# Local softmax's sums from a column of ones beside the values, one result tile of two banks, and GpSimd's value copies in eight pieces

## The chip, the cores and the metric

The kernel runs on one core of a Trainium2 chip. The metric is the time of one execution on the device, in microseconds (us). The engines are named as in the profile: PE is TensorE (PEld its weight loads), DVE is VectorE, ACT is ScalarE, POOL is GpSimd, SP is SyncE, which only issues DMAs here.

## The reference

Attention over 8 batches, 8 heads, 576 positions and 64 dimensions, in fp32; then a mixture of experts over the 4608 resulting rows of 512. Heads 0 to 3 are local (a row sees itself and the 31 positions before it), heads 4 to 7 are strided (a row sees earlier positions that are equal to it modulo 32).

```
scores = scale * np.matmul(q, k.transpose(0, 1, 3, 2))
mask_local = (rel >= 0) & (rel < stride)
mask_strided = (rel >= 0) & (pos[None, :] % stride == pos[:, None] % stride)
scores = np.where(masks[None, :, :, :], scores, -1000000000.0)
scores = scores - np.max(scores, axis=-1, keepdims=True)
attn = np.exp(scores)
attn = attn / (np.sum(attn, axis=-1, keepdims=True) + 1e-09)
out = np.matmul(attn, v)
...
logits = x @ w_gate
expert_idx = np.argmax(logits, axis=1)
...
    h = np.maximum(x_sorted[lo:hi] @ w1[e], 0.0)
    y_sorted[lo:hi] = h @ w2[e]
```

Each row of the expert stage is scaled by its gate's softmax weight and put back in its own place.

## The kernel before, in words

Attention takes roughly the first 235 us; the experts follow. Attention is a pipeline of 40 chunks, five in a batch, in the order strided, local, strided, local, local (list `ch`, line 650). A local chunk has 256 rows (the last of a batch 64) of the four local heads, in blocks of 32 rows that each see 64 keys: their own 32 and the 32 before. The loop of line 687 runs one step n for each chunk and interleaves the stages of neighbouring chunks; the order in which the code is written is the order on every engine, as nothing is reordered afterwards.

For a local chunk the stages are, with the step at which each stands relative to the chunk's own: scores (`qkl`, PE, one step ahead), row maxima and subtraction (`sml_a`, lines 306 and 307, DVE, one step ahead), the exponential (`sml_x`, line 312, ACT), the sums of the exponentials, 1e-9 and the reciprocals (`sml_b`, lines 317 to 319, DVE, at the end of the chunk's own step), transposes of the exponentials (`ptl`, line 326 on PE and 328 on ACT, one step later), the product with the values (`avl`, line 344 on PE, two steps later) and, on DVE, the result times the reciprocal into the row tile `xr` (line 349, one instruction for each parity of the heads). Three steps later `otl` transposes the rows for the gate (line 362 on PE, 364 on ACT) and `rows_out` adds the strided heads' columns (lines 377 and 378) and stores the rows. So line 349 is followed in the next step by line 362.

The strided chunks go through `sms_a` (lines 238, 239), `sms_x` (243), `sms_b` (248 to 253, which ends in DVE's transpose `pts`), `sms_c` (260 on DVE, 262 on ACT) and `avs` (273 on PE; 278 on DVE or 280 on ACT move its result).

The results of `avl` and `avs` both lie in PSUM tiles `o` of one bank each, two of them in turn. Transposes go through three PSUM tiles `t`, so a PE transpose can wait for whoever reads the tile used three allocations before.

The local values of a batch lie in `VL[b % 2]` (tile `vl` or `xg`): 18 blocks of 32 positions for each of two pairs of heads. A partition group holds the block's own keys (rows `own`) and the block before it (rows `prev`). `load_vl` brings the own rows by DMA, issued by SP; `load_prev` (line 120) lets POOL copy them, one block on, to the `prev` rows, with one copy of 2176 elements per parity, thus two a batch. In POOL's program these two copies stand after the ranking work of an earlier batch (lines 499 to 525) and before that of the next.

Once a batch, in the same step as `load_prev`, the ranking of an earlier batch begins: the gate's logits, transposed on PE (line 431), are summed on DVE (432, 440), DVE subtracts the maxima (442, tile `rw`), and ACT takes their exponential (444). On ACT this exponential stands ahead of line 328 of the running step. Later DVE steps of the ranking are 445 to 449 and 472 to 488; PE's part are lines 457 to 470 and 530. At the end of attention the last chunks are interleaved with the splits of the first expert's weights (573 on ACT, 574 on DVE), with padding counts (461 to 466), and with the first tiles of the experts, for which `hidden` also uses the PSUM tiles of attention.

Of the kernel before, what the change touches and what calls it, by code (L numbers as in the profile page):

```python
# [8 lines left out]
F32 = mybir.dt.float32  # L9
# [4 lines left out]
OP = mybir.AluOpType  # L14
# [9 lines left out]
DM = H * D  # L24
NTOK = B * S
# [15 lines left out]
def kernel(ctx, tc, q, k, v, w_gate, w1, w2, out):  # L41
# [7 lines left out]
    XA, XB = (keep.tile([128, n], F32, name=nm) for nm, n in (("x1", 4096), ("xg", 2 * NB * D)))  # L49
# [15 lines left out]
    VL = [p0.tile([128, 2, NB, D], F32, name="vl"),  # L65
# [41 lines left out]
    def load_vl(b):  # L107
        t = VL[b % 2]
        for par in range(2):

            own = slice(64 * par + 32, 64 * par + 64)
            for hp in range(2):
                nc.sync.dma_start(t[own, hp], bass.AP(tensor=v.tensor, offset=base(v, b, 2 * hp + par),
                                                      ap=[[D, 32], [32 * D, NB], [1, D]]))

    def load_prev(b):
        t = VL[b % 2]
        for par in range(2):
            own, prev = slice(64 * par + 32, 64 * par + 64), slice(64 * par, 64 * par + 32)
            G.tensor_copy(t[prev, :, 1:], t[own, :, :NB - 1])  # L120
# [50 lines left out]
    V.memset(VL[0][:, :, 0:1], 0.0)  # L171
# [10 lines left out]
    SC = psk.tile([128, 2, 2, 256], F32, name="sc")  # L182
    QTS, PS, PL, PT, OL, XS, XL, RL = ({} for _ in range(8))
# [80 lines left out]
    def avs(b, c):  # L264
# [3 lines left out]
        for hp in range(2):  # L268
            p = ps.tile([128, 4, 4, NB], F32, name="o", bufs=2)
# [30 lines left out]
    def sml_a(b, g):  # L300
        n = 8 if g < 2 else 4
        s = PL.pop((b, g)).rearrange("p a j h c -> p a (j h) c")
        mx = RL[b, g] = wk.tile([128, 8, 2], F32, name="mxl", bufs=4)
        p = PT[b, g] = wk.tile([128, 8, 64], F32, name="pl", bufs=3)
        two = lambda t: t[:, :n].rearrange("p (x a) c -> p a x c", a=2)
        V.tensor_reduce(two(mx)[:, :, :, 0], s, axis=AX.X, op=OP.max)
        V.tensor_tensor(two(p), s, two(mx)[:, :, :, 0:1].to_broadcast([128, 2, n // 2, 64]), op=OP.subtract)
# [5 lines left out]

    def sml_b(b, g):
        n = 8 if g < 2 else 4
        mx, p = RL[b, g], PT[b, g]
        V.tensor_reduce(mx[:, :n, 0], p[:, :n], axis=AX.X, op=OP.add)
        V.tensor_scalar(mx[:, :n, 0], mx[:, :n, 0], 1e-9, None, op0=OP.add)
        V.reciprocal(mx[:, :n, 1], mx[:, :n, 0])
# [11 lines left out]
    def avl(b, g):  # L331
# [3 lines left out]
        mx = RL.pop((b, g))  # L335
        o = OL[b, g] = wk.tile([128, 2, DM], F32, name="xr", bufs=3)
        ps2 = [ps.tile([128, 2, 2, D], F32, name="o", bufs=2) for par in range(2)]
        for jj in range(nj):
            for hp in range(2):
                for j in range(nq):  # L340
                    blk = 8 * g + 4 * jj + j
                    for par in range(2):
                        r = slice(64 * par, 64 * par + 64)
                        T.matmul(ps2[par][32 * j:32 * j + 32, jj, hp], pt[r, 2 * jj + hp, 32 * j:32 * j + 32],  # L344
                                 VL[b % 2][r, hp, blk], start=True, stop=True)
            if jj == 0: yield
        for par in range(2):
            rs = mx.rearrange("p (j a h) e -> p j a h e", a=2, h=2)[:rows, :nj, :, par, 1:2]
            V.tensor_tensor(o[:, :, :4 * D].rearrange("p j (a h d) -> p j a h d", a=2, h=2)[:rows, :nj, :, par], ps2[par][:rows, :nj],
                            rs.to_broadcast([rows, nj, 2, D]), op=OP.mult)  # L350
# [336 lines left out]
    for n in range(-1, N + 3):  # L687
# [26 lines left out]
        if n == 0:  # L714
            V.memset(VL[1][:, :, 0:1], 0.0)
# [42 lines left out]
        at(n, sms_b, sml_b)  # L758
# [25 lines left out]
    def hidden():  # L784

        for f in range(8):
            p = ps.tile([128, C0], F32, name="o", bufs=2) if f % 2 else SC[:, f // 2 % 2, 0]
# [71 lines left out]
    z = [ps.tile([TM, DM], F32, name="o", bufs=2) for t in range(N0)]  # L859
# [235 lines left out]
```

## Time and profile before

| | |
|---|---|
| median of 3 runs | 692.95 us |
| lowest, highest run | 689.67, 693.1 us |
| the profiled execution | 693.73 us, of which the span of its instructions is 691.9 us |
| mean granted TensorE clock | 0.971 |
| busy share PE, DVE, ACT, POOL over the span | 92%, 50%, 44%, 28% |
| a full batch of attention (113.6 to 137.7 us) | PE 21.82, DVE 21.32, ACT 16.32, POOL 10.81 of 24.10 us |

All lines of the trace are from the one profiled execution. A row of the timeline reads: start in us from the span's start, duration in us, engine, line, operation, output and inputs by the names of the tiles with shapes, how many instructions are merged into the row, and in square brackets how long the engine sat idle before it and for whom. "issue" there means that the profile shows nothing that was waited for. A row of groups reads: line, engine, operation, tiles, shapes, count | busy us in all, mean ns of one | idle time before them. A row of the windows gives the length of a stretch and the busy time of each engine in it, then the granted clock, the share of the DMA engines and GB/s.

### The profile page before, as it was taken

What the parts mean: (1) busy time and instruction counts of PE and PEld (TensorE: products, weight loads), DVE (VectorE), ACT (ScalarE), POOL (GpSimd) and SP (SyncE); (2) the same over time, 40 slices, a digit from 0 to 9 for tenths busy, and PEclk for the clock granted to TensorE, in tenths of its full rate; (3) what the DMA queues carried; (4) which work ended last, traced back from release to release, by engine and by line L of the source; (5) the groups of instructions that cost most, each with busy time, mean ns of one, the idle gap of its engine ahead of it and who ended that gap; (6) DMA issues with size and microseconds to landing.
All of it is one profiled execution on the core that took longest, in us unless ns stands there. A gap on an engine that the chain in (4) does not pass through costs nothing.

```text
span 691.9 us, 18307 instructions
## 1 busy us (share of the span) xinstructions
PE 637.9 (92%) x7558; PEld 552.7 (80%) x7558; DVE 345.3 (50%) x766; ACT 307.2 (44%) x596; POOL 196.6 (28%) x263
## 2 busy tenths in 40 slices
PE   6678989988977989999999999999998999999995
PEld 4556666766656869999899799889997998999994
DVE  5866889886898653343334243443331542414210
ACT  6547756764764342433433243432441542434211
POOL 0222245425435570060140060141043041103002
PEclk9899999999996999999999999999999999999998
DMA  8898677868655271380470470561435343231001
GB/s 189 182 212 206 173 204 184 216 183 187 145 182 164 71 267 42 93 282 22 162 224 1 140 247 29 164 206 31 139 97 185 99 144 122 66 108 68 17 17 56
DMA packets 91029, 95.59 MB, mean 138 GB/s; under 512 B 62158, under 2 KB 64206, under 8 KB 90833
## 3 DMA queue, kind: packets, MB, share of 16 engines
q1 hardware_dynamic: 83152, 71.34, 37.6%
q0 software_dynamic: 7680, 22.03, 9.1%
q8 instruction: 75, 1.23, 0.8%
q14 instruction: 122, 0.99, 0.5%
HBM read 74.47 MB, written 22.02 MB: 139 GB/s over the span
## 4 chain that ended last, share of the span: by engine, by line
PE 70%; issue 11%; DVE 7%; ACT 5%; DMA 3%; POOL 2%; SPq 2%; POOLq 0%; ACTq 0%; DVEq 0%
PE h L623 8%; PE h L625 8%; PE h L624 8%; PE y L641 5%; PE y L642 5%; PE y L643 5%; PE t L613 2%; PE y L897 2%; PE y L895 2%; PE y L896 2%; PE t L201 2%; PE o L273 2%; PE o L344 2%; PE z L641 2%; PE z L642 2%
## 5 line engine op out<-in xcount | busy, mean ns | idle before, releaser
L884 POOL DMA_INDIRECT out_dram<-yo,idx x48 | 54.8, 1142 | 293.8 <-ACT yo L647 176.7
L630 DVE SCALAR_TENSOR_TENSOR h1l<-h,h1h 128x256 fp32r<-128x256 f32 (+3 forms) x64 | 32.8, 512 | 122.7 <-ACT h1h L629 122.7
L623 PE MATMUL h<-x,w1h 128*128 128x256 f32 (+3 forms) x256 | 82.2, 321 | 0.8 <-ACT yo L647 0.8
L625 PE MATMUL h<-x,w1l 128*128 128x256 f32 (+3 forms) x256 | 80.9, 316 | 0.0
L624 PE MATMUL h<-x,w1h 128*128 128x256 f32 (+3 forms) x256 | 80.9, 316 | 0.0
L629 ACT ACTIVATE h1h<-h 128x256 fp32r<-128x256 f32 (+3 forms) x64 | 29.1, 454 | 104.7 <-PE h L625 88.0
L603 POOL DMA_INDIRECT xg<-xrows,src x48 | 53.7, 1118 | 49.7 <-PE h L623 29.7
L623 PE MATMUL h<-x0h,w1h 128*128 128x256 f32 x224 | 63.6, 284 | 0.3 <-ACT yo L647 0.3
L624 PE MATMUL h<-x0l,w1h 128*128 128x256 f32 x224 | 63.4, 283 | 0.0
L625 PE MATMUL h<-x0h,w1l 128*128 128x256 f32 x224 | 63.4, 283 | 0.0
L630 DVE SCALAR_TENSOR_TENSOR h0l<-h,h0h 128x256 fp32r<-128x256 f32 x56 | 23.3, 420 | 72.3 <-ACT h0h L629 72.3
L574 DVE TENSOR_TENSOR w1l<-stg,w1h 128x1024 fp32r<-128x1024 f32 x32 | 38.7, 1229 | 24.6 <-ACT w1h L573 24.6
L623 PEld LDWEIGHTS h<-x,w1h 128*128 128x128 f32 x256 | 48.1, 188 | 1.6 <-issue 1.2
L624 PEld LDWEIGHTS h<-x,w1h 128*128 128x128 f32 x256 | 48.1, 188 | 0.3
L625 PEld LDWEIGHTS h<-x,w1l 128*128 128x128 f32 x256 | 48.0, 188 | 0.0
L580 DVE TENSOR_TENSOR w<-stg,w 128x1024 fp32r<-128x1024 f32 x32 | 38.9, 1221 | 12.4 <-ACT w L579 12.4
L623 PEld LDWEIGHTS h<-x0h,w1h 128*128 128x128 f32 x224 | 42.9, 192 | 0.9 <-ACT yo L647 0.5
L624 PEld LDWEIGHTS h<-x0l,w1h 128*128 128x128 f32 x224 | 42.9, 192 | 0.3
L625 PEld LDWEIGHTS h<-x0h,w1l 128*128 128x128 f32 x224 | 43.0, 192 | 0.0
L647 ACT ACTIVATE yo<-y,gw 128x512 f32<-128x512 f32 (+2 forms) x26 | 17.8, 685 | 51.7 <-PE y L643 47.0
L641 PE MATMUL y<-w,h1h 128*128 128x512 f32 (+1 forms) x96 | 38.9, 406 | 0.0
L895 PE MATMUL y<-h1h,w 128*128 128x288 f32 (+1 forms) x128 | 38.6, 301 | 0.0
(243 smaller groups left out, 1592.5 us busy)
## 6 DMA issues: line engine op xcount, KB each, us to landing
stg<-in_moe_w_dram SPq DMA_DIRECT2D x64, 512.0 KB
xrows<-xr SPq DMA_DIRECT2D x16, 512.0 KB
qs<-in_q_dram SPq DMA_DIRECT2D x8, 512.0 KB
ks<-in_k_dram SPq DMA_DIRECT2D x8, 512.0 KB
ql<-in_q_dram SPq DMA_DIRECT2D x32, 128.0 KB
kl<-in_k_dram SPq DMA_DIRECT2D x32, 128.0 KB
vs<-in_v_dram SPq DMA_DIRECT2D x16, 144.0 KB
vl<-in_v_dram SPq DMA_DIRECT2D x16, 144.0 KB
```

The source lines that it names most:

```text
L574: V.tensor_tensor(l[:, i], t, h[:, i].bitcast(F32), op=OP.subtract)
L580: V.tensor_tensor(l, t, h.bitcast(F32), op=OP.subtract)
L603: G.indirect_dma_start(out=XG[t], out_offset=None, in_=x_out[:rows, :], in_offset=bass.IndirectOffsetOnAxis(ap=src[:, NT * e + t:NT * e + ...
L623: T.matmul(p, W1H[:, c, fs], x[0][:, c, :n], start=(c == 0), stop=False)
L624: T.matmul(p, W1H[:, c, fs], x[1][:, c, :n], start=False, stop=False)
L625: T.matmul(p, W1L[:, c, fs], x[0][:, c, :n], start=False, stop=(c == 3))
L630: V.scalar_tensor_tensor(h[1][:, f, :n], p, 0.0, h[0][:, f, :n].bitcast(F32), op0=OP.max, op1=OP.subtract)
L641: T.matmul(p, h[0][:, f, cs], W2H[:, f], start=(f == 0), stop=False)
L642: T.matmul(p, h[1][:, f, cs], W2H[:, f], start=False, stop=False)
L643: T.matmul(p, h[0][:, f, cs], W2L[:, f], start=False, stop=(f == 7))
L884: i = G.indirect_dma_start(out=out, out_offset=bass.IndirectOffsetOnAxis(ap=idx[:, c:c + 1], axis=0), in_=YO[t], in_offset=None, bounds_ch ...
L895: T.matmul(p, W2H[:, f, ds_], H1[0][:, f, cs], start=(f == 0), stop=False)
```

## The change

Three things are changed, all around the local heads' product with the values.

1. A value row gets a 65th element that is one (`DV = D + 1`). `VL` has rows of 65; the ones are written once by a memset for each of the two tiles, and the DMAs bring only the first 64. The product's moving operand has 65 columns, so its last column is the sum of the exponentials. `sml_b` is gone, with its three DVE instructions per local chunk. In `avl`, between the product and the two multiplications, DVE now adds 1e-9 to the sums in PSUM (one instruction for both parities) and takes the reciprocals.
2. The two PSUM tiles `o` become one tile `oo` of two banks that is held throughout; the strided product, `hidden` and the first expert's `z` take its halves in the same turn as before.
3. `load_prev` makes eight copies a batch, of nine or eight blocks (585 or 520 elements), in place of two of 2176.

```
+DV = D + 1
...
-    XA, XB = (keep.tile([128, n], F32, name=nm) for nm, n in (("x1", 4096), ("xg", 2 * NB * D)))
+    XA, XB = (keep.tile([128, n], F32, name=nm) for nm, n in (("x1", 4096), ("xg", 2 * NB * DV)))
...
-    VL = [p0.tile([128, 2, NB, D], F32, name="vl"),
+    VL = [p0.tile([128, 2, NB, DV], F32, name="vl"),
...
-                nc.sync.dma_start(t[own, hp], bass.AP(tensor=v.tensor, offset=base(v, b, 2 * hp + par),
+                nc.sync.dma_start(t[own, hp, :, :D], bass.AP(tensor=v.tensor, offset=base(v, b, 2 * hp + par),
...
-            G.tensor_copy(t[prev, :, 1:], t[own, :, :NB - 1])
+            for hp in range(2):
+                for j in (1, 10):
+                    n = min(9, NB - j)
+                    G.tensor_copy(t[prev, hp, j:j + n], t[own, hp, j - 1:j + n - 1])
...
-    V.memset(VL[0][:, :, 0:1], 0.0)
+    V.memset(VL[0][:, :, 0:1, :D], 0.0)
+    V.memset(VL[0][:, :, :, D:], 1.0)
...
+    OO = psk.tile([128, 2, 512], F32, name="oo")
...
-            p = ps.tile([128, 4, 4, NB], F32, name="o", bufs=2)
+            p = OO[:, hp, :16 * NB].rearrange("p (e x i) -> p e x i", e=4, x=4)
...
-    def sml_b(b, g):
-        n = 8 if g < 2 else 4
-        mx, p = RL[b, g], PT[b, g]
-        V.tensor_reduce(mx[:, :n, 0], p[:, :n], axis=AX.X, op=OP.add)
-        V.tensor_scalar(mx[:, :n, 0], mx[:, :n, 0], 1e-9, None, op0=OP.add)
-        V.reciprocal(mx[:, :n, 1], mx[:, :n, 0])
...
-        ps2 = [ps.tile([128, 2, 2, D], F32, name="o", bufs=2) for par in range(2)]
+        ps2 = OO[:, :, :4 * DV].rearrange("p a (j h d) -> p a j h d", j=2, h=2)
...
-                        T.matmul(ps2[par][32 * j:32 * j + 32, jj, hp], pt[r, 2 * jj + hp, 32 * j:32 * j + 32],
+                        T.matmul(ps2[32 * j:32 * j + 32, par, jj, hp], pt[r, 2 * jj + hp, 32 * j:32 * j + 32],
                                  VL[b % 2][r, hp, blk], start=True, stop=True)
...
+        rs = wk.tile([128, 2, 2, 2, 2], F32, name="rs")
+        sm, rc = rs[:rows, 0, :, :nj], rs[:rows, 1, :, :nj]
+        V.tensor_scalar(sm, ps2[:rows, :, :nj, :, D], 1e-9, None, op0=OP.add)
+        V.reciprocal(rc, sm)
         for par in range(2):
-            rs = mx.rearrange("p (j a h) e -> p j a h e", a=2, h=2)[:rows, :nj, :, par, 1:2]
-            V.tensor_tensor(o[:, :, :4 * D].rearrange("p j (a h d) -> p j a h d", a=2, h=2)[:rows, :nj, :, par], ps2[par][:rows, :nj],
-                            rs.to_broadcast([rows, nj, 2, D]), op=OP.mult)
+            V.tensor_tensor(o[:, :, :4 * D].rearrange("p j (a h d) -> p j a h d", a=2, h=2)[:rows, :nj, :, par],
+                            ps2[:rows, par, :nj, :, :D], rc[:, par, :, :, None].to_broadcast([rows, nj, 2, D]), op=OP.mult)
...
-        at(n, sms_b, sml_b)
+        at(n, sms_b, None)
...
-            p = ps.tile([128, C0], F32, name="o", bufs=2) if f % 2 else SC[:, f // 2 % 2, 0]
+            p = OO[:, f // 2 % 2, :C0] if f % 2 else SC[:, f // 2 % 2, 0]
...
-    z = [ps.tile([TM, DM], F32, name="o", bufs=2) for t in range(N0)]
+    z = [OO[:, t] for t in range(N0)]
```

The first place where the order moves is DVE, in the step whose local result is transposed on PE right after it; `xr` is that result's row tile, `mxl` and `rs` hold maxima, sums and reciprocals, and `sc` the next scores. Before:

```order
L306 TENSOR_REDUCE mxl<-sc 128x2x2
L307 TENSOR_TENSOR pl<-sc,mxl 128x2x2x64
L349 TENSOR_TENSOR xr<-o,mxl 128x2x2x64 x2
L317 TENSOR_REDUCE mxl<-pl 128x8
L318 TENSOR_SCALAR mxl<-mxl 128x8
L319 RECIPROCAL mxl<-mxl 128x8
L238 TENSOR_REDUCE mxs<-sc 128x16
```

And on DVE at the same place in the changed kernel, whose lines are numbered up to seven higher here:

```order
L313 TENSOR_REDUCE mxl<-sc 128x2x2
L314 TENSOR_TENSOR pl<-sc,mxl 128x2x2x64
L348 TENSOR_SCALAR rs<-oo 128x8
L349 RECIPROCAL rs<-rs 128x8
L351 TENSOR_TENSOR xr<-oo,rs 128x2x2x64 x2
L244 TENSOR_REDUCE mxs<-sc 128x16
```

The sum and its two small companions behind the multiplications are gone, and two small instructions of their kind stand ahead of the multiplications instead.

The second place is DVE a few rows on, where the ranking begins (`lgo` and `rt` are the logits and their maxima, `rw` the difference that ACT waits for). Before:

```order
L278 COPY xs<-o 128x72x4
L317 TENSOR_REDUCE mxl<-pl 128x4
L318 TENSOR_SCALAR mxl<-mxl 128x4
L319 RECIPROCAL mxl<-mxl 128x4
L432 TENSOR_REDUCE lgo<-t 96x24 x2
L440 TENSOR_REDUCE rt<-lgo 96x6
L442 TENSOR_TENSOR rw<-lgo,rt 96x48
```

And on DVE there in the changed kernel:

```order
L284 COPY xs<-oo 128x72x4
L434 TENSOR_REDUCE lgo<-t 96x24 x2
L442 TENSOR_REDUCE rt<-lgo 96x6
L444 TENSOR_TENSOR rw<-lgo,rt 96x48
L313 TENSOR_REDUCE mxl<-sc 128x2x4
```

Three instructions between the copy of the strided result and the logits are gone, so the logits follow the copy at once.

The third place is POOL at the end of a batch's ranking, where `ohacc` is the running count and `xg` the tile of local values. Before:

```order
L513 TENSOR_TENSOR bp<-b_2619,pay 96x6x48 x5
L525 TENSOR_TENSOR ohacc<-ohacc,oh 96x8 x6
L120 COPY xg<-xg 32x2x1088 x2
L499 TENSOR_TENSOR d_3170<-g_3110 96x36
L501 TENSOR_TENSOR b_3171<-oh,d_3170 96x288
```

And on POOL there in the changed kernel:

```order
L527 TENSOR_TENSOR ohacc<-ohacc,oh 96x8 x5
L124 COPY xg<-xg 32x585
L124 COPY xg<-xg 32x520
L124 COPY xg<-xg 32x585
L124 COPY xg<-xg 32x520
L124 COPY xg<-xg 32x585
L124 COPY xg<-xg 32x520
L124 COPY xg<-xg 32x585
L124 COPY xg<-xg 32x520
L501 TENSOR_TENSOR d_2058<-g_2000 96x36
```

Two long copies have become eight short ones at the same place of the queue.

More of the change, by code (lines that the diff above doesn't have):

```diff
@@ L302, in sml_a @@
         s = PL.pop((b, g)).rearrange("p a j h c -> p a (j h) c")
-        mx = RL[b, g] = wk.tile([128, 8, 2], F32, name="mxl", bufs=4)
+        mx = wk.tile([128, 8], F32, name="mxl")
         p = PT[b, g] = wk.tile([128, 8, 64], F32, name="pl", bufs=3)
         two = lambda t: t[:, :n].rearrange("p (x a) c -> p a x c", a=2)
-        V.tensor_reduce(two(mx)[:, :, :, 0], s, axis=AX.X, op=OP.max)
-        V.tensor_tensor(two(p), s, two(mx)[:, :, :, 0:1].to_broadcast([128, 2, n // 2, 64]), op=OP.subtract)
+        two1 = mx[:, :n].rearrange("p (x a) -> p a x", a=2)
+        V.tensor_reduce(two1, s, axis=AX.X, op=OP.max)
+        V.tensor_tensor(two(p), s, two1[:, :, :, None].to_broadcast([128, 2, n // 2, 64]), op=OP.subtract)
     def sml_x(b, g):
@@ L334, in avl @@
         pt = PTT.pop((b, g))
-        mx = RL.pop((b, g))
         o = OL[b, g] = wk.tile([128, 2, DM], F32, name="xr", bufs=3)
-        ps2 = [ps.tile([128, 2, 2, D], F32, name="o", bufs=2) for par in range(2)]
+        ps2 = OO[:, :, :4 * DV].rearrange("p a (j h d) -> p a j h d", j=2, h=2)
         for jj in range(nj):
@@ L714 @@
         if n == 0:
-            V.memset(VL[1][:, :, 0:1], 0.0)
+            V.memset(VL[1][:, :, 0:1, :D], 0.0)
+            V.memset(VL[1][:, :, :, D:], 1.0)
             V.memset(BD[0], 0.0)
```

## The prediction

> **What bounds the kernel now.** I read the page first, then the windows batch by batch, then the timeline of one full batch of attention with its waits. The change touches only attention, so its batches are the stage to read. A full batch, and the two after it, in the windows:
>
> ```profile
> 113.60:137.70 24.10, 21.82 (x594) 16.09 (x593) 21.32 (x58) 16.32 (x38) 10.81 (x20) 1.00 0.83 209
> 162.10:188.60 26.50, 25.24 (x668) 19.09 (x668) 20.90 (x61) 17.90 (x41) 10.81 (x20) 0.97 0.69 171
> 188.60:212.00 23.40, 18.31 (x486) 12.78 (x484) 21.51 (x55) 12.87 (x28) 11.20 (x17) 0.91 0.41 144
> ```
>
> In the first of these PE is busy 21.82 of 24.10 us and DVE 21.32: neither bounds it alone, and whatever DVE gives up, PE has only 24.10 - 21.82 = 2.28 us of idle time to hand back. In the second PE has 1.26 us; the last batch is DVE's (21.51 of 23.40). The timeline shows where the idle time of the full batch lies. Around the two value copies of POOL:
>
> ```profile
> 113.31 0.41 DVE L317 TENSOR_REDUCE mxl<-pl 128x4 f32<-128x256 f32 x1
> 113.62 4.04 POOL L120 COPY vl<-vl 32x2176 f32<-32x2176 f32 x2
> 113.75 1.88 DVE L318 TENSOR_SCALAR mxl<-mxl 128x4 f32<-128x4 f32 x1
> 115.67 0.18 DVE L319 RECIPROCAL mxl<-mxl 128x4 f32<-128x4 f32 x1
> 115.76 0.39 DVE L432 TENSOR_REDUCE lgo<-t 96x24 f32<-96x96 f32 x2
> 116.04 0.44 PE L189 MATMUL t<-ident,ql 128*128 128x128 f32 x2 [0.93 <-DVE lgo L432]
> 116.49 1.23 DVE L442 TENSOR_TENSOR rw<-lgo,rt 96x48 f32<-96x48 f32 x1
> 117.75 0.24 ACT L444 ACTIVATE rw<-rw 96x48 f32<-96x48 f32 x1 [4.91 <-DVE rw L442]
> 118.31 0.66 PE L377 MATMUL t<-ident,xs 128*128 128x128 f32 x4 [0.26 <-ACT ptl L328]
> ```
>
> L318 handles eight columns at most and takes 1.88 us; it ends at 115.63, where the first of two copies of 2.02 us ends (113.62 + 2.02 = 115.64). L442 ends at 117.72, where the second one does. So DVE stands still for POOL twice. Behind L442 waits ACT (4.91 us), behind ACT's line 328 waits PE (0.26), and behind L432 PE (0.93): 1.19 us of PE's idle time, and the rest of it follows further on. Undisturbed, L442 takes what it takes in the last batch, and these are the groups:
>
> ```profile
> 215.36 0.20 DVE L442 TENSOR_TENSOR rw<-lgo,rt 96x48 f32<-96x48 f32 x1
> L317 DVE TENSOR_REDUCE mxl<-pl 128x8 f32<-128x512 f32 (+1 forms) x24 | 14.0, 584 | 0.0
> L318 DVE TENSOR_SCALAR mxl<-mxl 128x8 f32<-128x8 f32 (+1 forms) x24 | 12.5, 520 | 0.8
> L319 DVE RECIPROCAL mxl<-mxl 128x8 f32<-128x8 f32 (+1 forms) x24 | 4.7, 195 | 0.8
> ```
>
> Not every batch pays: where PE itself stalled before the copies, L318 and L442 hold nobody up. In the batch at 162 us L442 is back to 0.20. The batches that begin at 89.5, 113.6, 137.7 and 188.6 show the pattern above in full.
>
> **What goes.** 24 sums of 584 ns, 14.0 us of DVE, and 24 small pairs from their old place, L318's blocked time with them (12.5 us, where 24 times the quiet 0.17 us would be 4.1). That is a relief for DVE and not yet for the kernel. In the pattern, L432 follows the copy of the strided result directly, about 2.3 us earlier (from 113.31 to 115.76 less its own wait for PE), and finds PE's logits only just there; L442 can then start near 114.4. It still has two inputs in SBUF and still meets POOL, now with a short piece.
>
> Groups of POOL's copies of 2176 elements and of one of 8, and what POOL does after the copies:
>
> ```profile
> L120 POOL COPY vl<-vl 32x2176 f32<-32x2176 f32 x8 | 15.9, 1992 | 38.9 <-PE o L273 20.1 <-DMA vl<-in_v_dram 18.6
> L523 POOL COPY ohacc<-oh 96x8 bf16<-96x8 bf16 x1 | 0.2, 183 | 0.0
> 126.32 0.24 POOL L499 TENSOR_TENSOR d<-g 96x36 bf16<-96x36 f32 x1 [8.67 <-DVE g L478]
> ```
>
> A straight line through both gives 0.83 ns an element and 0.18 us fixed, so 0.66 us for 585 elements and 0.61 for 520: eight pieces are 5.1 us and with gaps some 5.4, where there were 4.04. POOL's 1.4 us more lie in idle time (line 499 comes at 126.32, after 8.67 us of idling). A DVE instruction that meets a piece waits at most 0.66 us. Three do, L442, L445 and L449, on average half a piece each, 1.0 us together; the scores that L306 needs after them are only ready at 116.2 by PE's own time, so the last two are hidden. L442 then ends by 115.1 and not at 117.72, ACT is free 2.6 us sooner, and both waits of PE vanish: **1.19 us** a batch.
>
> The Trainium skill says under "SBUF — State Buffer", section "Who interferes with whom", that a DVE instruction with two SBUF inputs, or in a mode that uses both port pairs, and a GpSimd one exclude each other for a whole instruction, and that at most one SBUF input outside such a mode does not contend. The trace agrees on the first (L318's 1.88 us, L442's 1.23). By the second the new addition, which reads PSUM, would never meet POOL, which no run shows yet; the sum is the same without it. Against the change speaks "GPSIMD Engine Reference", section 2, whose table puts a fixed dispatch cost before every POOL instruction; the 183 ns of the copy of 8 elements is its size here, and it is in the 1.4 us above.
>
> **What is added.** Two dependent small DVE instructions stand between product and multiplications, in 24 places. The nearest rows are the strided heads' pair with its user, and the one addition that reads PSUM:
>
> ```profile
> 120.88 0.17 DVE L249 TENSOR_SCALAR mxs<-mxs 128x16 f32<-128x16 f32 x1
> 121.09 0.25 DVE L250 RECIPROCAL mxs<-mxs 128x16 f32<-128x16 f32 x1
> 121.38 0.46 DVE L251 TENSOR_TENSOR w<-w,mxs 128x288 f32<-128x288 f32 x1
> 219.76 0.14 DVE L463 TENSOR_SCALAR pd<-t 1x1 f32<-1x1 f32 x1
> ```
>
> From L249's start to L251's are 0.50 us with 16 columns; with 8, L319's 0.195 in place of 0.25, and an addition like L463's, it is 0.41. Bounds: 0.33 (the two durations alone) and 0.50; I take 0.42. It counts where the result is waited for:
>
> ```profile
> 109.77 0.75 DVE L349 TENSOR_TENSOR xr<-o,mxl 128x256 f32<-128x256 f32 x2 [0.16 <-PE o L344]
> 110.69 0.66 PE L362 MATMUL t<-ident,xr 128*128 128x128 f32 x4
> 118.90 0.46 PE L344 MATMUL o<-xg,ptl 64*32 64x64 f32 x32
> 119.28 0.34 PE L189 MATMUL t<-ident,ql 64*128 64x64 f32 x2
> 119.74 0.75 DVE L349 TENSOR_TENSOR xr<-o,mxl 128x256 f32<-128x256 f32 x2
> 122.61 0.91 ACT L262 ACTIVATE w<-pts 32x288 f32<-32x288 f32 x2 [0.66 <-DVE pts L253]
> 124.19 0.18 PE L457 MATMUL t<-oh,upper 96*96 96x48 bf16 x1 [0.52 <-ACT qts L207]
> 127.04 0.69 DVE L306 TENSOR_REDUCE mxl<-sc 128x8 f32<-128x512 f32 x1 [0.86 <-PE sc L296]
> ```
>
> At 109.77 DVE has been waiting for PE, its pair ends at 110.52, and PE takes it up at 110.69, busy until then; 0.14 of the 0.17 us between I count as slack. So 0.42 - 0.14 = **0.28 us** of new wait on PE, once a batch, with PE at full clock: five batches (L362 at 61, 86, 110, 135 and 186 us), 1.4 us. In the other batches PE is slower or starting, and it hides.
>
> At 119.74 DVE is late, not PE (the product ended at 119.36). With PE 1.19 earlier the product ends at 118.17, plus 0.1 for the signal and 0.42 puts the multiplications at 118.69, **1.05 us** earlier. From there the chain is as it was: L248 to L253, ACT's 262 and 207, PE's 457. At 127.04 DVE waits for PE again, so the third pair, at 124.13, and the removed sum behind it, are both off the path.
>
> The last batch starts with the same 1.05. Then DVE is saturated up to 208 us, saves one sum with its pair (1.03) and adds two pairs, and after that PE waits for DVE right behind L349 three times, each with a new 0.42 in front; two of these rows, and PE's gap before them, are
>
> ```profile
> 206.17 0.38 PE L344 MATMUL o<-xg,ptl 64*32 64x64 f32 x18 [1.50 <-issue]
> 208.54 1.12 PE L362 MATMUL t<-ident,xr 128*128 128x128 f32 x4 [1.41 <-DVE xr L349]
> 220.13 0.20 PE L466 MATMUL t<-padv,ones 96*96 96x48 bf16 x1 [1.91 <-DVE padv L464]
> ```
>
> -1.05 - 1.03 + 2 x 0.42 leaves -1.2 at 207, of which PE's issue gap at 206 takes some 0.5; -0.4 after the addition at 219, 0 to -0.3 after the one at 224. I take **-0.2**.
>
> **The 65th column.** 1,152 products of 64 columns, in runs of 32 that hold PE 0.385 us (118.90 to 119.28): 36 runs, 13.9 us, and 1/64 more is 0.2 us. The nearest products:
>
> ```profile
> L344 PE MATMUL o<-xg,ptl 64*32 64x64 f32 x576 | 9.9, 225 | 3.6 <-issue 3.6
> L273 PE MATMUL o<-w,vs 128*64 128x72 f32 x256 | 10.7, 231 | 0.0
> ```
>
> Line 273's with 72 columns take 231 ns, line 344's with 64 take 225, so nothing larger is in sight. The two memsets of ones (36 elements) lie in DVE's start-up: 0.1 us at most. The common tile `oo` changes no bank's turn: both parities of line 344 always waited for both. It is 0.
>
> **The sum.** Three full batches x 1.05 = 3.15, last batch 0.2; against it 1.4 + 0.2 + 0.1. Net -1.65 us on the profiled execution of 693.73 (span 691.9): 692.1. That execution lies 0.8 above the median, so 692.95 - 1.65 = **691.3 us**. With the pair at 0.33 it is 690.5, at 0.50 691.9.
>
> **Rivals.** (a) *DVE was the bound after all.* Then all PE idle time of the three batches goes, 3 x 2.28 - 0.8 = 6.0, and the last, DVE-saturated one keeps 1.0 of what it saves: 693 - 7 = 686 us. For it: DVE is busy 21.32 of 24.10 us, and the end of attention is DVE's. Against it: PE's other two idle pieces, 0.52 at 124.19 and the row
>
> ```profile
> 130.17 0.44 PE L189 MATMUL t<-ident,ql 128*128 128x128 f32 x2 [0.40 <-ACT w L211]
> ```
>
> have ACT ahead of them, which nothing here relieves. Chance 0.25.
>
> (b) *DVE does not get in between POOL's pieces.* If POOL's next piece always goes first, L442 waits until 113.62 + 5.4 = 119.0 and not 117.72, ACT's 444 and 328 and PE's 377 with it: +1.3 in four batches, +1.4 and +0.5 as above, 692.95 + 7 = 700 us in the worst case, and slower from about two pieces of waiting beyond the old end. Against it: L318 ended with the first copy while the second was already queued. Chance 0.06.
>
> (c) *The values land at rows of 260 bytes.* All local values come as packets of 256 bytes:
>
> ```profile
> q1 hardware_dynamic: 83152, 71.34, 37.6%
> vl<-in_v_dram SPq DMA_DIRECT2D x16, 144.0 KB
> ```
>
> 691.9 x 16 x 0.376 / 83152 is 50 ns a packet; a batch has 4 x 576 of them, 7.2 us of the 16 engines, in a batch whose DMA share is already 0.83 (20 of 24.1 us). Half as much again would be +3.6 and fill the batch: slower by up to 2 us in each of six, 703 us. No row shows a packet with such a start; the bounds are 0 and +7.2 us (a packet counted twice). I take 0, since nothing in the trace separates packets by address. The Trainium skill ("DMA: Bandwidth & Descriptors", section "How a descriptor splits into AXI transactions") lets a descriptor that does not start at a multiple of 256 bytes pay for the bytes from the boundary below. It speaks of reads, which here stay as they were; no run shows whether writes follow it. Chance 0.07.
>
> (d) *It does nothing*: L442 stays as late because DVE is held elsewhere, and the additions are hidden too: 693 us. Chance 0.05.
>
> **How the numbers follow.** The forecast has 0.57, its own range 689 to 694. A measurement tells about 0.5% from no change (the three runs span 3.4 us), 3.5 us here. The forecast gives 0.48 same, 0.07 faster, 0.02 slower; (a) 0.25 faster; (b) and (c) 0.01 same, 0.12 slower; (d) 0.05 same. So faster 0.32, same 0.54, slower 0.14. The range reaches from 685 (a, a little beyond) to 697 (b with half its price); what lies outside is (c), part of (b) and the tail of (a).
>
> **What would show it.** Right: no row of a small DVE instruction above 0.9 us around POOL's pieces; L442 within 0.7 of its quiet 0.20; PE's waits for `lgo` and for ACT's `ptl` gone; a batch period of some 23.3 us in place of 24.1; a new wait of 0.2 to 0.3 of PE's transposes for `xr` once a batch. Wrong: a period under 22.5 (a), L442 of 2 us or more (b), a DMA share above 0.95 with more gaps of PE that nothing explains (c), or a period of 24.1 (d).

## The result and the profile after

The changed kernel takes **698.81 us** (median of 6 runs, 697.81 to 700.81) where the kernel before takes 692.05 (6 runs, 689.67 to 694.37): ratio 1.0106 [1.0074, 1.0137], slower by about 7 us. The forecast was 691.3, the range 685 to 697. The profiled execution took 697.81 us, its span is 696.0. The medians given in us are of all executions, while the ratios and their intervals leave out those more than 1.5 per cent above the fastest of their kernel, which are none here and none to two of each kernel below, but six of the twelve of rows260_only.

Line numbers of the changed kernel are some higher: 120 is now 124, 273 to 280 are 279 to 286, 344 is 343, 349 is 351, 362 is 364, 442 to 445 are 444 to 447, 457 is 459, 603 is 605, 623 to 630 are 625 to 632; the late pair is 348 and 349. Each experiment's kernel has a numbering of its own.

First the windows of the changed kernel, a full batch and the last (columns as before the change: stretch, length, busy time of PE, PEld, DVE, ACT and POOL, granted clock, DMA share, GB/s):

```profile
113.15:137.86 24.71, 21.74 (x595) 16.24 (x594) 17.91 (x55) 17.12 (x38) 11.66 (x27) 1.00 0.82 201
188.84:213.81 24.97, 20.24 (x509) 14.58 (x508) 19.07 (x62) 13.10 (x28) 11.56 (x25) 0.90 0.45 155
```

DVE has lost 3.4 us a batch (21.32 to 17.91) and PE does the same work as before (21.74 us against 21.82), yet the batch is 0.6 us longer: PE idles 2.97 us where it idled 2.28. In the last batch, from the sixth reduction of `lgo` to the seventh, DVE is busy 19.07 of 24.97 us where it was 21.39 of 23.66, and PE idles 4.73 us where it idled 4.45. DVE has time to spare, and PE gains nothing by it. The timeline of the same place as before the change, around POOL's copies, shows what PE waits for:

```profile
111.47 0.41 ACT L286 ACTIVATE xs<-oo 128x288 f32<-128x288 f32 x1 [0.45 <-PE oo L279]
111.67 4.90 POOL L124 COPY vl<-vl 32x585 f32<-32x585 f32 x8
111.93 0.72 PE L279 MATMUL oo<-w 128*64 128x72 f32 x16 [0.51 <-ACT xs L286]
113.15 0.58 DVE L434 TENSOR_REDUCE lgo<-t 96x24 f32<-96x96 f32 x2
114.08 0.20 DVE L444 TENSOR_TENSOR rw<-lgo,rt 96x48 f32<-96x48 f32 x1
114.31 0.24 ACT L446 ACTIVATE rw<-rw 96x48 f32<-96x48 f32 x1 [2.43 <-DVE rw L444]
117.93 0.17 DVE L348 TENSOR_SCALAR rs<-oo 128x8 f32<-128x8 f32 x1 [0.53 <-PE oo L343]
118.13 0.20 DVE L349 RECIPROCAL rs<-rs 128x8 f32<-128x8 f32 x1
118.37 0.76 DVE L351 TENSOR_TENSOR xr<-oo,rs 128x256 f32<-128x256 f32 x2
128.09 0.72 PE L279 MATMUL oo<-w,vs 128*64 128x72 f32 x16 [0.93 <-ACT xs L286]
```

What the change was to remove is gone: L444 takes 0.20 and not 1.23 us, and is done at 114.28, long before POOL (116.57). ACT waits 2.43 in place of 4.91. From L348's start to L351's are 0.44 us. But the products of line 279 stop twice in a batch, 0.51 and 0.93 us, until ACT has copied the result of the *other* bank. Before, line 273's second half never waited for that:

```profile
111.66 1.22 PE L273 MATMUL o<-w 128*64 128x72 f32 x32
112.43 0.41 ACT L280 ACTIVATE xs<-o 128x288 f32<-128x288 f32 x1 [0.45 <-PE o L273]
```

ACT copied the first bank from 112.43 on, and PE's run of 32 products, the second 16 of them into the other bank, went on without a stop to 112.88.

The groups of the small instructions and of the copies (busy time, mean ns, idle time before):

```profile
L124 POOL COPY vl<-vl 32x585 f32<-32x585 f32 (+1 forms) x32 | 19.6, 648 | 34.5 <-DMA vl<-in_v_dram 34.2
L348 DVE TENSOR_SCALAR rs<-oo 128x8 f32<-128x8 f32 (+1 forms) x24 | 3.8, 159 | 11.8 <-PE oo L343 6.2 <-ACT ls L395 5.6
L444 DVE TENSOR_TENSOR rw<-lgo,rt 96x48 f32<-96x48 f32 x8 | 1.7, 207 | 0.3
```

To compare kernels I use a stretch of equal work: from the first reduction of `lgo` (line 432 of before) in the first batch to that of the seventh. PE's waits in it, in the kernel before (from 66.02 to 214.45 us; total, times, longest):

```profile
PE o L344 <- issue: 3.6, 3, 1.7
PE t L189 <- DVE lgo L432: 3.6, 4, 0.9
PE t L457 <- ACT qts L207: 2.5, 4, 0.7
PE t L362 <- DVE xr L349: 1.4, 1, 1.4
PE t L377 <- ACT ptl L328: 0.8, 3, 0.3
```

and in the changed one (63.6 to 213.81):

```profile
PE oo L279 <- ACT xs L286: 7.7, 11, 0.9
PE t L459 <- ACT qts L213: 4.6, 5, 1.1
PE t L364 <- DVE xr L351: 3.1, 5, 1.4
PE oo L343 <- issue: 2.9, 3, 1.4
```

The 4.4 us for `lgo` and `ptl` are gone. In their place stand 7.7 for `xs`, and the waits for `qts` and `xr` have grown from 3.9 to 7.7. ("issue" is time in which PE waits for nothing that the profile shows.)

The largest loss lies after attention. The second lot of gathers, which feeds the experts (its first is the third gather in all), starts at 241.95 us before and here at 247.34; from there to the end of the span it is 449.95 and 448.66 us. So this profiled execution lost its time ahead of that gather. Before the change PE's last `inv` product and the gather stand at

```profile
238.75 0.79 PE L530 MATMUL inv<-bp,a 96*128 96x240 bf16 x6 [0.77 <-POOL ohacc L525]
241.95 1.02 POOL L603 DMA_INDIRECT xg<-xrows,src  x1 [2.10 <-DVE idx L594]
```

and in the changed kernel, PE and DVE and POOL together:

```profile
238.16 0.28 PE L627 MATMUL sc<-x0h,w1l 128*128 128x256 f32 x1
238.66 2.15 DVE L515 TENSOR_TENSOR bp<-b,pay 96x288 bf16<-96x288 bf16 x3
241.94 0.41 DVE L632 SCALAR_TENSOR_TENSOR h0l<-oo,h0h 128x256 fp32r<-128x256 f32 x1
242.40 0.39 PE L625 MATMUL oo<-x0h,w1h 128*128 128x256 f32 x1 [3.96 <-DVE h0l L632]
244.65 1.42 PE L532 MATMUL inv<-bp,a 96*128 96x240 bf16 x6
246.97 0.20 DVE L596 SCALAR_TENSOR_TENSOR idx<-ivs,gw 128x46 int32<-128x46 f32 x1
247.34 1.02 POOL L605 DMA_INDIRECT xg<-xrows,src  x1 [4.51 <-DVE idx L596]
```

PE wants to fill bank 0 of `oo` with the experts' block 5. It waits 3.96 us for DVE's reading of block 3, which lies in bank 1 and comes late because DVE is busy with the last batch's ranking. Behind PE's block 5 is queued `inv`, and behind that the gather's list: 244.65 and 247.34.

The stop is not all of the 5.4 us. The windows from the seventh reduction of `lgo` to the eighth, and from there to the gather, before:

```profile
214.45:228.73 14.28, 10.61 (x147) 8.29 (x146) 10.13 (x29) 7.50 (x14) 8.09 (x14) 0.75 0.76 227
228.73:241.95 13.22, 12.03 (x110) 11.43 (x109) 10.34 (x38) 3.42 (x9) 6.19 (x21) 1.00 0.02 7
```

and in the changed kernel:

```profile
213.81:230.62 16.81, 13.02 (x148) 9.61 (x147) 10.85 (x32) 7.69 (x14) 9.17 (x19) 0.64 0.67 196
230.62:247.34 16.72, 12.76 (x105) 12.10 (x104) 10.48 (x38) 3.38 (x8) 4.94 (x16) 0.90 0.01 1
```

The second stretch, with the stop in it, is 3.5 us longer; after the stop the granted clock is 0.65 until the gather (242.40 to 247.34). The first is 2.5 us longer, and there PE is busy 13.02 us with the work that took 10.61, at a granted clock of 0.64 against 0.75. The profile lists no wait for the other bank in that first stretch.

### The profile page after: what moved, and what is told of

It is laid out like the page before. It is cut to its first block, busy times and chain, and to the rows that moved or that the text cites. A ratio compares the mean times of both kernels' runs of the same rounds, so it can differ in the third digit from the quotient of the medians.

```text
span 696.0 us, 18351 instructions
## 1 busy us (share of the span) xinstructions
PE 635.2 (91%) x7558; PEld 551.4 (79%) x7558; DVE 323.6 (46%) x744; ACT 310.7 (45%) x596; POOL 202.0 (29%) x311
## 3 DMA queue, kind: packets, MB, share of 16 engines
q1 hardware_dynamic: 83152, 71.34, 37.7%
q8 instruction: 75, 1.23, 0.8%
## 4 chain that ended last, share of the span: by engine, by line
PE 72%; issue 10%; DVE 7%; ACT 4%; SPq 2%; POOL 2%; DMA 1%; POOLq 0%; ACTq 0%; DVEq 0%
PE h L625 8%; PE h L626 8%; PE h L627 8%; PE y L643 5%; PE y L644 5%; PE y L645 5%; PE oo L279 2%; PE t L615 2%; PE sc L302 2%; PE y L900 2%; PE y L898 2%; PE y L899 2%; PE oo L343 2%; PE z L643 2%; DVE xr L351 2%
## 5 line engine op out<-in xcount | busy, mean ns | idle before, releaser
L626 PE MATMUL h<-x0l,w1h 128*128 128x256 f32 x224 | 63.6, 284 | 1.3 <-issue 1.3
L625 PE MATMUL h<-x0h,w1h 128*128 128x256 f32 x224 | 63.6, 284 | 0.0
L898 PE MATMUL y<-h1h,w 128*128 128x288 f32 (+1 forms) x128 | 38.7, 303 | 0.0
L900 PE MATMUL y<-h1h,w 128*128 128x288 f32 (+1 forms) x128 | 38.6, 301 | 0.0
```

Source lines behind the costliest of these rows:

```text
L625: T.matmul(p, W1H[:, c, fs], x[0][:, c, :n], start=(c == 0), stop=False)
L626: T.matmul(p, W1H[:, c, fs], x[1][:, c, :n], start=False, stop=False)
L898: T.matmul(p, W2H[:, f, ds_], H1[0][:, f, cs], start=(f == 0), stop=False)
L900: T.matmul(p, W2L[:, f, ds_], H1[0][:, f, cs], start=False, stop=(f == 7))
```

## The experiments

All ratios are to the kernel before, run on the same chip beside each (its medians 692.7 to 693.4 us). My theory after the result: the program orders accesses by tile, so one tile of two banks makes each bank wait for the readers of the other; the rival: the sums' late place, or the column, costs the time. The first four kernels take the change apart. The expectations call the first "theory of the common tile".

### The tile's two banks, made independent

**halves_free**: the changed kernel, with the accesses of the two banks declared independent wherever `oo` is used.

```diff
+    def of(k, i, rd=0):                       # k: bank, rd: a reader
+        for x in HALF[1 - rd][1 - k]:
+            tc.declare_no_dep(i.ins, x, reason="the other bank")
+        HALF[rd][k].append(i.ins)
...
-                    T.matmul(p[64 * par:64 * par + 64, e]..., start=True, stop=True)
+                    of(hp, T.matmul(p[64 * par:64 * par + 64, e]..., start=True, stop=True))
```

> The changed kernel, except that nothing waits any more between the two banks of the result tile: PE's products into one bank no longer wait for ACT's or DVE's read of the other, in attention, in the fill of the first expert and in its second product. Theory of the common tile: the time goes back below the kernel before, to 688 to 692 us, a batch of attention takes 23.0 to 23.8 us, and PE's wait of 4.0 us for DVE near 242 us is gone. Rival, the late sums (addition and reciprocal ahead of the multiplications): 696 to 699 us, as the changed kernel. Rival, value rows of 260 bytes that slow the DMAs: 697 to 699 us.

Measured: 693.93 us, ratio 1.0005 [0.9972, 1.0038], against 1.0106 for the changed kernel: 7 us come back with no other edit, and PE's wait of 4 us is gone. The time itself lies between the theory's range (688 to 692 us) and the rivals' (from 696), and the batches are not the 23.0 to 23.8 us expected: the first five between `lgo` reductions take 24.42 to 25.78. So the tile is the loss, and without its waits the gain that was forecast still does not appear. Its timeline at the place where the changed kernel stopped:

```profile
111.05 1.22 PE L287 MATMUL oo<-w 128*64 128x72 f32 x32
111.81 0.41 ACT L294 ACTIVATE xs<-oo 128x288 f32<-128x288 f32 x1 [0.45 <-PE oo L287]
```

The 32 products run through in 1.22 us while ACT reads the first bank. The order between the banks was the program's, not the chip's. The Trainium skill advises, under "PSUM — Partial Sum Buffer", section "Summary: rules for kernel authors", that what is read while a matmul runs lie in a different bank, and that semaphores guard by bank. These rows agree: 1.22 us without a stop, where guarding the tile as a whole had put 0.51 us between two halves of 0.72.

**two_tiles**: the changed kernel with two single-bank tiles in turn, as before the change; one addition for each parity.

```diff
-        ps2 = OO[:, :, :4 * DV].rearrange("p a (j h d) -> p a j h d", j=2, h=2)
+        ps2 = [ps.tile([128, 2, 2, DV], F32, name="o", bufs=2) for par in range(2)]
...
-        V.tensor_scalar(sm, ps2[:rows, :, :nj, :, D], 1e-9, None, op0=OP.add)
+        for par in range(2):
+            V.tensor_scalar(sm[:, par], ps2[par][:rows, :nj, :, D], 1e-9, None, op0=OP.add)
```

> The changed kernel with two PSUM tiles in turn, as before, and one addition for each parity instead of one for both (0.2 us more on DVE in 24 places). Theory of the common tile: 689 to 693 us. Rivals (late sums, rows of 260 bytes): 697 to 700 us.

Measured: 693.91 us, ratio 1.0017 [0.9988, 1.0045], 0.9 us above the theory's range and 3 below the rivals'. Without the common tile the rest of the change makes no difference that can be told.

**one_tile_only**: the kernel before, with its two `o` tiles made one tile of two banks and nothing else.

```diff
-            p = ps.tile([128, 4, 4, NB], F32, name="o", bufs=2)
+            p = OO[:, hp, :16 * NB].rearrange("p (e x i) -> p e x i", e=4, x=4)
...
-    z = [ps.tile([TM, DM], F32, name="o", bufs=2) for t in range(N0)]
+    z = [OO[:, t] for t in range(N0)]
```

> The kernel before with nothing changed but the two result tiles made one of two banks. Theory of the common tile: 698 to 703 us, with PE's products of the strided heads waiting for ACT twice a batch and 4 us near 240 us. Rivals: 692 us, within 1 us of the kernel before.

Measured: 695.12 us, ratio 1.0037 [1.0005, 1.0068]. PE's waits from 60 to 262 us show the two that the changed kernel has:

```profile
PE oo L274 <- ACT xs L281: 8.2, 12, 0.9
PE oo L624 <- DVE h0l L631: 4.1, 2, 4.0
```

So the waits come with the tile alone. They cost less here than in the changed kernel: the time lies between the two expectations (698 to 703 and 692 us), and the second lot of gathers starts at 244.04, 2.1 us later than before and not 5.4. The two stretches ahead of it show where the difference lies, from the seventh reduction of `lgo` to the eighth and from there to the gather:

```profile
213.87:227.75 13.88, 10.73 (x146) 8.23 (x146) 10.15 (x30) 7.70 (x14) 8.26 (x14) 0.77 0.75 232
227.75:244.04 16.29, 12.33 (x101) 11.67 (x100) 10.48 (x38) 3.38 (x8) 6.34 (x21) 0.90 0.03 10
```

The stop costs much the same as in the changed kernel (16.29 and 16.72 us, 13.22 before). The stretch ahead of it is not longer here: 13.88 us at a granted clock of 0.77, against 16.81 at 0.64. What lowers the clock there in the changed kernel is not settled; the same tile alone did not.

### The pieces alone

**pieces_only**: the kernel before with the eight short copies.

```diff
-            G.tensor_copy(t[prev, :, 1:], t[own, :, :NB - 1])
+            for hp in range(2):
+                for j in (1, 10):
+                    n = min(9, NB - j)
+                    G.tensor_copy(t[prev, hp, j:j + n], t[own, hp, j - 1:j + n - 1])
```

> The kernel before with nothing changed but the value copies in eight pieces. Theory of the common tile, with the prediction's price of the blocked DVE instructions: 689 to 692 us, line 318 and line 442 below 0.9 us. Rivals: they say nothing of it; if the blocked DVE was hidden anyway, 692 us.

Measured: **688.82 us**, ratio 0.9938 [0.9899, 0.9976]: faster than both kernels, 0.2 us below the expected range, and no row of the two lines above 0.55 us. PE's waits from the first `lgo` to the seventh (63.51 to 208.24):

```profile
PE t L460 <- ACT qts L210: 2.1, 4, 0.6
PE t L365 <- DVE xr L352: 1.7, 1, 1.7
```

No wait for `lgo` or for `ptl` is left, and two of its batches took 22.64 and 23.01 us. What stands between this kernel and two_tiles, 0.8 per cent, is the column of ones with the sums behind the product. The next runs look for which part.

### The late pair

**late_after_product**: pieces_only, with addition and reciprocal moved behind the product, and the addition waiting for it.

```diff
-        V.tensor_scalar(mx[:, :n, 0], mx[:, :n, 0], 1e-9, None, op0=OP.add)
-        V.reciprocal(mx[:, :n, 1], mx[:, :n, 0])
...
+        for par in range(2):
+            V.scalar_tensor_tensor(sm(par, 0), ps2[par][:rows, :nj, :, 0], 0.0, sm(par, 0), op0=OP.mult, op1=OP.add)
+        V.reciprocal(mx[:rows, :n, 1], mx[:rows, :n, 0])
```

> The kernel before with the eight pieces; the sums stay with DVE's reduction, products of 64 columns, rows of 256 bytes, two tiles in turn. Only the pair is moved: the addition (zero times a result in PSUM plus the sum, in place of 1e-9 plus the sum) and the reciprocal stand between the product and the multiplications and wait for the product. Theory L (the late pair makes DVE's answer to PE 0.42 us later at every product, and PE pays for it through its transposes for xr, through the chain of DVE's 251 to 263 and ACT to PE's line 460 and in the next product): the ratio to before rises from the pieces' 0.994 to 1.000 to 1.004 (693 to 695 us), PE's wait at line 460 in a full batch goes from 0.2 to 0.9 or more, and 0.4 appears at the transposes for xr. Theory R (the rows of 260 bytes, or the 65th column, take back what the pieces gave): 0.992 to 0.997, PE's wait at line 460 below 0.5.

Measured: 692.48 us, ratio 0.9984 [0.9947, 1.0021]. PE's waits between the same two points (65.23 to 212.37):

```profile
PE t L368 <- DVE xr L355: 4.9, 7, 2.4
PE t L463 <- ACT qts L210: 4.4, 4, 1.1
```

By the waits theory L holds: 3.8 us have become 9.3. By the time the point lies between the ranges of L (1.000 to 1.004) and R (0.992 to 0.997): +0.46 per cent against the pieces alone, where L expected 0.6 to 1.0, and the two intervals overlap.

**late_pair**: the same, but the pair works on DVE's own sum and waits for nothing of PE.

```diff
+        n = 8 if g < 2 else 4
+        V.tensor_scalar(mx[:, :n, 0], mx[:, :n, 0], 1e-9, None, op0=OP.add)
+        V.reciprocal(mx[:, :n, 1], mx[:, :n, 0])
         for par in range(2):
```

> The kernel before with the eight pieces; addition and reciprocal stand in the late place, directly ahead of the multiplications, but work on DVE's own sum and so do not wait for PE's product. Theory W (what costs is that the pair waits for the product): where DVE idles ahead of the product the pair is done by then; PE's waits for xr and at line 460 stay near the pieces' 1.7 and 2.1 us between the first batch and the seventh, ratio 0.992 to 0.998. Theory P (what costs is only the place of 0.42 us of work in DVE's order): as late_after_product, waits of about 4.9 and 4.4 us, ratio 0.997 to 1.002.

Measured: 692.70 us, ratio 0.9980 [0.9954, 1.0005], at the edge of both theories, and the time of late_after_product (0.9984). Its waits (62.69 to 211.78) lie between:

```profile
PE t L366 <- DVE xr L353: 2.3, 2, 1.8
PE t L366 <- ACT pl L315: 1.9, 3, 0.6
PE t L461 <- ACT qts L210: 1.5, 3, 0.6
```

The wait for `qts` did not grow (W), the transposes of `xr` wait 4.2 in place of 1.7 (P, in part). How much is the place of the pair and how much its waiting is not settled.

**two_tiles_noadd**: two_tiles without the addition of 1e-9; the reciprocal reads PSUM.

```diff
-            V.tensor_scalar(sm[:, par], ps2[par][:rows, :nj, :, D], 1e-9, None, op0=OP.add)
-        V.reciprocal(rc, sm)
+            V.reciprocal(rc[:, par], ps2[par][:rows, :nj, :, D])
```

> The changed kernel with two result tiles in turn and without the additions of 1e-9 (the greatest term of each sum is 1, so the addition changes no digit): the reciprocal reads PSUM itself, twice, one for each parity. It leaves out that addition and nothing else. Between product and multiplications some 0.25 us stand less. Theory L: PE's waits for xr and at line 459 shrink by about 0.2 each in a full batch, 1.5 to 2.5 us in all: ratio to before 0.998 to 1.000 against 1.0017 with the additions. Theory R: no change, 1.001 to 1.003.

Measured: 691.57 us, ratio 0.9991 [0.9960, 1.0021]. The point value lies in theory L's range, and PE's wait for `qts` fell from two_tiles' 4.4 us to 2.9 while the one for `xr` stayed at 2.9; two_tiles' interval contains the ratio all the same.

### The column, its rows, and the pieces beside it

**rows260_only**: pieces_only with values at rows of 65 elements, filled with ones but not used; products of 64 columns.

```diff
-    VL = [p0.tile([128, 2, NB, D], F32, name="vl"),
+    VL = [p0.tile([128, 2, NB, DV], F32, name="vl"),
...
+                                 VL[b % 2][r, hp, blk, :D], start=True, stop=True)
```

> The kernel before with the eight pieces, and the values at rows of 65 elements (260 bytes) with the column of ones filled and copied, but products of 64 columns and the sums by DVE as before. Theory R (rival c of the prediction, the values' transfers are slower at such rows): ratio to before 1.000 or more, DMA share of a full batch above 0.9, mean packet time above 50 ns. Theory L (the late pair): as with the pieces alone, 0.990 to 0.997 (686 to 691 us), DMA share as before, about 0.8.

Measured: 692.99 us over all twelve executions, level with the 692.8 of the kernel before; ratio 0.9924 [0.9881, 0.9967], as the pieces alone, but on six of them. The DMA share of two of its full batches is 0.89 and 0.88, below theory R's 0.9 and above theory L's 0.8. This run by itself does not settle it; the next has the same rows.

**product65_only**: the same with products of 65 columns; the 65th result is not used.

```diff
-                                 VL[b % 2][r, hp, blk, :D], start=True, stop=True)
+                                 VL[b % 2][r, hp, blk], start=True, stop=True)
```

> The kernel before with the eight pieces, rows of 260 bytes and products of 65 columns, whose 65th result is not used: sums and pair by DVE in the early place as before. Two result tiles in turn. Theory L (the late pair is the cost): 0.2 to 0.6 us for the column, ratio 0.991 to 0.998. Theory C (the 65th column itself is dear, in PE's products or in the multiplications' reading of results at rows of 260 bytes): 0.998 or more, with the product's run of 32 above 0.40 us or the multiplication above 0.45 us each.

Measured: 690.15 us, ratio 0.9951 [0.9917, 0.9986]: theory L, and neither the column nor its rows cost anything that can be told; theory R's 1.000 lies outside the interval. The queue of the input transfers (packets, MB, share of 16 engines' span), in pieces_only:

```profile
q1 hardware_dynamic: 83152, 71.34, 38.5%
```

and in product65_only:

```profile
q1 hardware_dynamic: 83152, 71.34, 38.2%
```

684.4 x 16 x 0.385 / 83152 is 50.7 ns a packet, and 691.1 x 16 x 0.382 / 83152 is 50.8. In rows260_only it is 692.1 x 16 x 0.386 / 83152 = 51.4. Local values are 8 x 4 x 576 = 18,432 of the packets; half as much again for each of them would have raised the mean by 5 to 6 ns. So rows of 260 bytes at the destination change little or nothing.

**two_tiles_long**: two_tiles with the two long copies.

```diff
-            for hp in range(2):
-                for j in (1, 10):
...
+            G.tensor_copy(t[prev, :, 1:], t[own, :, :NB - 1])
```

> The changed kernel with two result tiles in turn and the two long copies of values in place of the eight pieces: the column of ones alone. If the pieces give their 0.6 per cent here too: ratio to before 1.006 to 1.010 (697 to 699 us), with DVE's line 444 at 1.2 us again. If the pieces have nothing left to give once the sums are off DVE (the late pair sets the pace in any case): 1.000 to 1.003, as with the pieces.

Measured: 696.10 us, ratio 1.0053 [1.0024, 1.0082]; the line that is 444 in the changed kernel takes 0.75 to 0.97 us in four batches, and the one behind it, 447 there, takes 2.04 us in the same four (0.56 beside the pieces): without the sums ahead of it, another instruction meets the long copy. Both expectations missed by a little: the pieces give 0.36 per cent here against 0.62 alone, which would be part of their gain; the intervals of this kernel and of two_tiles overlap. The column and the late sums without the pieces are a loss by themselves.

### Where the common tile costs

**halves_free_end** frees the two banks only in the experts' first layer and in `z`; **halves_free_avs** only in attention.

```diff
 # halves_free_end
+        on(k, A.activation(h[0][:, f, :n], p, AF.Relu), 1)
+        on(k, V.scalar_tensor_tensor(h[1][:, f, :n], p, 0.0, h[0][:, f, :n].bitcast(F32), op0=OP.max, op1=OP.subtract), 1)
...
 # halves_free_avs
+                of(hp, A.activation(dst, p.rearrange("p e x i -> p i x e"), AF.Copy), 1)
```

> The changed kernel; accesses of the two banks of the common tile are declared independent of each other only where the experts' first layer (hidden) and the results z use it; in attention the tile stays as in the changed kernel. With both freed the ratio to before was 1.0005, with neither 1.0106. Theory E (the common tile's price lies at the end, where the queue of the second lot's gathers starts 5.4 us later because PE waits 4 us for DVE in the other bank): 0.999 to 1.004 (692 to 696 us), third gather near 242 us. Theory A (it lies in attention, where PE waits 7.7 us for ACT's copies of xs between the 66th and the 214th us): 1.006 to 1.011, third gather near 242 all the same.

> The counterpart: the two banks are declared independent only in attention (the strided heads' and the local products); hidden and z stay as in the changed kernel. Theory E: PE's 7.7 us of waits for xs go, but other waits take most of their place, and the third gather stays near 247 us: ratio 1.005 to 1.010. Theory A: 0.999 to 1.004, since 7.7 us are 1.1 per cent.

Measured: 694.48 us, ratio 1.0031 [0.9997, 1.0065] for the end freed; 701.57 us, ratio 1.0130 [1.0089, 1.0171] for attention freed. Theory E holds for the first, and the second misses its range on the far side of theory A: what can be told of the price lies at the end. In the former, `inv` and gather stand where they stood before the change, or earlier:

```profile
237.14 0.79 PE L540 MATMUL inv<-bp,a 96*128 96x240 bf16 x6 [0.76 <-POOL ohacc L535]
240.34 1.02 POOL L613 DMA_INDIRECT xg<-xrows,src  x1 [2.10 <-DVE idx L604]
```

and in the latter the stop of 3.96 us is still there:

```profile
241.64 0.39 PE L633 MATMUL oo<-x0h,w1h 128*128 128x256 f32 x1 [3.96 <-DVE h0l L640]
246.39 1.02 POOL L613 DMA_INDIRECT xg<-xrows,src  x1 [4.32 <-DVE idx L604]
```

From the eighth reduction of `lgo` to this gather are 13.21 or 13.22 us in every kernel of this document whose banks do not wait for each other at the end, and 16.29 to 16.72 in the three where they do (the changed kernel, one_tile_only, halves_free_avs): the stop costs 3.1 to 3.5 us. The low granted clock ahead of it is in two of these three alone: from the seventh reduction to the eighth halves_free_avs has 17.00 us at 0.63, the changed kernel 16.81 at 0.64, and all others 13.88 to 15.22 at 0.74 to 0.89.

PE's 7.7 us of waits for `xs` in attention cost nothing that can be told: from the first `lgo` to the seventh are 148.57 us with them (halves_free_end) and 148.34 without (halves_free_avs). One execution shows no more than that, since the changed kernel, with the same attention as halves_free_end, took 150.21. Freed of them, PE stood longer elsewhere (6.3 us of "issue" in place of 3.1) and its mean granted clock was 0.98 in place of 1.00.

## Why the prediction was wrong, step by step

**POOL's copies hold DVE, and the pieces free it: right.** The small rows came out as named (L444 0.20, no row above 0.9), the waits for `lgo` and `ptl` are gone (4.4 us), and the pieces alone give 0.62 per cent, 4.3 us, where the sum had 3.35 (which has one delay by the late pair taken off already). Eight pieces took 4.90 us, 5.4 were forecast. The prediction let three DVE instructions meet a piece; L447 shows it (0.56 us), L444 no longer does. It left open whether an addition that reads PSUM waits for POOL: in two_tiles_long two of them start at 42.73 us inside a long copy (41.49 to 43.52) and take 0.23 us together, so there they do not. The period of some 23.3 us did not come: 24.71 in the changed kernel, and 24.42 to 25.78 in halves_free, whose banks are free. (The table that the prediction places in section 2 of the Trainium skill's "GPSIMD Engine Reference" stands in section 3.1.)

**"The common tile `oo` changes no bank's turn: both parities of line 344 always waited for both. It is 0."** This step failed, and with it the forecast. It is true of line 344, whose two banks are filled and read together, and only line 344 was looked at. Two other users of the tile fill one bank while the other is read: the strided heads' products (line 273) and the experts' first layer (lines 623 to 630). There the two banks stopped each other. Its measured size is 1.0106 against 1.0005, 7 us, of which 5.2 are the end (1.0106 against 1.0031). The traces show 3.1 to 3.5 us of these as the stop of PE for DVE's reading of the other bank; about 2 more go with the low granted clock ahead of it, whose cause stays open, and the rest is within the intervals. The tile alone, without that clock, cost 0.37 per cent, 2.6 us (one_tile_only). The trace of before could have shown the danger: none of PE's waits there is for ACT's `xs`, and the rows at 111.66 and 112.43 show line 273 filling the second bank while ACT reads the first. That overlap was what the tile took away.

**The late pair, 0.28 us once a batch, 1.4 in all, and "from there the chain is as it was": a mis-sized term.** The pair itself is 0.44 us (forecast 0.42). But PE pays for it in two places: its transposes for `xr`, and line 459, which waits for ACT's `qts` at the end of the chain that starts with the multiplications. In two_tiles these two waits sum to 7.3 us between the first batch and the seventh, in the kernel before to 3.9, with the pieces alone to 3.8: 3.5 us more, not 1.4. By the times, the pair behind the product costs 0.46 per cent, 3.2 us (0.9984 against 0.9938), on intervals that overlap; with a pair that does not wait for the product it is 0.42 (0.9980), so the place alone may be what costs.

**The 65th column, 0.2 us, is not contradicted, and rival (c) fell.** 0.9951 with columns and rows of 65, 0.9938 without; 0.2 us are too few to be seen in this. The Trainium skill's rule on descriptors ("DMA: Bandwidth & Descriptors", section "How a descriptor splits into AXI transactions") is on reads; the packets of 50.8 ns, 50.7 with rows of 256 bytes, show nothing of it for writes.

**Rivals (a), (b) and (d)** did not come either: DVE gave up 3.4 us a batch and no time came of it; DVE gets in between the pieces; and the change did do what it says.

**The sum by measured parts.** Pieces -0.62 per cent, column and late sums +0.79 (two_tiles against pieces_only), common tile +0.89 (the changed kernel against two_tiles): +1.06, or 7.4 us. The first two nearly cancel, as the prediction's own sum did in small; the third was not in it. These parts are made to add up, as each is the step from one kernel to the next. That column and late sums together cost 0.79 and their parts as measured add up to less (0.46 for the pair, nothing certain for the column) stays open within the intervals of about 0.35 each.

## What to carry to other kernels

When two buffers become one tile, look at every user of the tile for one that fills the first half while another engine reads the second, not only at the user for which they were joined: the program orders by tile, and here that cost more than the edit's gain (0.89 per cent against 0.62). Work moved behind a product is paid for at every later wait on the chain that starts there; follow the chain to where PE waits next before you call the rest of it unchanged. Of a change with three parts, run each part alone: here one was a gain (0.9938), and the sum a loss.

## What the runs showed of the chip that was not expected

Freed time did not come back whole. With the pieces two batches in a row took 23.01 and 22.64 us, the next two 25.83 and 27.13, with PE gaps that wait for nothing in the profile and a lower granted clock. The windows of pieces_only from one `lgo` reduction to the next:

```profile
86.52:109.16 22.64, 21.82 (x595) 16.22 (x594) 20.13 (x58) 16.66 (x38) 11.59 (x27) 1.00 0.82 203
109.16:134.99 25.83, 23.30 (x594) 17.21 (x593) 19.98 (x58) 16.53 (x38) 12.16 (x28) 0.93 0.78 202
```

The same 594 products hold PE 1.48 us longer at a clock of 0.93. Gaps of this kind sum to 3.1 to 8.3 us from the first `lgo` to the seventh, 5.7 in the kernel before and 6.9 here, and sit at other places in each kernel; the least (3.1 to 4.3) stand in the three kernels where PE waits for `xs`. What causes them was not tried.
